# A gate argument in one VectorE step, and a new order of the work, in a fused scan and mixture-of-adapters kernel

## The chip, the cores and the metric

The kernel runs on one core of a Trainium2 chip. The metric is the device time of one execution, in microseconds, as the median of several runs. The profile is one execution taken by the hardware profiler; the engines are named PE (TensorE), DVE (VectorE), ACT (ScalarE), POOL (GpSimd) and SP (the queue that issues the loads and stores).

## The reference

Two steps are computed one after the other. A linear recurrence runs over 8 sequences of 6400 steps with 128 channels, and its outputs, 51,200 rows x of 128 values, are the tokens of a small mixture of adapters with 8 experts of rank 16, of which the two with the largest logits count:

```python
h = a[:, t] * h + b[:, t]          # scan; x[:, t] = h
logits = x @ w_gate                # [N, 8]
topk = the two largest of 8; w = softmax over these two
out = x + sum over the two of w * ((x @ A[e]) @ B[e])
```

A softmax over two logits m1 >= m2 is sigmoid(m1 - m2) for the first and sigmoid(m2 - m1) for the second. With l a logit of the row, both are sigmoid((l - m1) + (l - m2)), and for the six other experts the gate must be 0. The kernel therefore makes a gate argument that is (l - m1) + (l - m2) for the two chosen experts and hugely negative for the rest, and takes one sigmoid of it.

## The kernel before

The 51,200 rows are cut into 100 units of 512 rows. A unit w passes through these operations, whose names are those in the code:

- `ld`: SP loads a and b, mostly two units (512 KB) in one transfer, into rings of 8 slots, that is 16 units.
- `AB` (line 492): PE transposes a and b, so that channels lie on partitions and time along the free axis, into one PSUM bank each. `aev` (L526): ACT copies the bank of a to SBUF. `scan` (L550): DVE runs the recurrence, with a from SBUF and b from PSUM.
- `ZL` (L589): PE multiplies x with w_gate and A together, 136 columns for each 128 rows, three such blocks in one PSUM bank. `zl` (L607): ACT copies logits and products to SBUF.
- the gating, for a group of several units at once (below).
- `mul` (L766): the products times the gates, on POOL, 128x512, for all units but the last few, where the planner may choose DVE. `T` (L774): PE transposes the result; `tev` (L782): a copy from PSUM, on DVE in the middle of the kernel. `D` (L802): PE adds x and the product with B. `oev` (L817): ACT copies the output to SBUF. `st`: SP stores two units at a time; the store of unit u also waits for the scan of unit u + 20 (`HOLD`).

The gating of a group (the function `gating`, with tiles of 4 blocks of 8 logits for each unit of the group, so 128x96 for three units) is a chain of short operations on three engines: `m1` (DVE, largest logit), `p1` (POOL, d1 = l - m1), `r1` (ACT, a mask pn that is huge where l is the largest), `p3` (POOL, L2 = l - pn), `m2` (DVE, second largest), `p4` (POOL, d2 = l - m2), `r2` (ACT, a mask pn that is huge where l < m2), `p6` (POOL, d1 + d2), `p7` (POOL, um = d1 - pn), `sig` (ACT, g = sigmoid(um)). The first two and the last two groups are "quick": one operation per block on DVE (`mx`, L662) gives the eight logits sorted, so that m1, r1, p3 and m2 fall away, and the p steps may go to POOL or DVE.

The order in which each engine executes its instructions is not written by hand. A planner (`_Plan.schedule`) gives every operation a duration, and repeatedly picks the operation that can start first by these durations, with the `key` table of the configuration to decide between equals. Where an operation may run on two engines, it takes the one on which it starts earlier by the planner's durations. The planner also hands out the eight PSUM banks; `caps` says how many of them may be held at once by a (transposed a), b, Z (products) and O (output). Each engine then executes its list strictly in order and waits on semaphores of the other engines.

Of the kernel before, what the change touches and what calls it, by code (L numbers as in the profile page):

```python
# [5 lines left out]
ALU = mybir.AluOpType  # L6
ACTF = mybir.ActivationFunctionType
# [5 lines left out]
CFG = {  # L13
    "ring": 8,
    "xr": 20,
    "zr": 48,
    "nout": 24,
    "hold": 20,
    "heads": (1, 1, 1, 1),
    "group": 3,  # L20
    "tails": (2, 2, 1, 1),
    "quick": (2, 2),
    "split": (4, 4),
    "solo": (0, 2),
    "mul": (0, 1, 0, 8),
    "tev": (1, 1, 4, 4),
    "tail": 8,
    "fills": 5,
    "caps": {'a': 3, 'b': 4, 'Z': 1, 'O': 3, 'w': 8},
    "least": {'Z': 1, 'O': 1},  # L30
    "pairs": (98, 2),
    "ast": 3,
    "tevns": (264.0, 330.0),
    "key": {
        "AB": 170.4, "aev": 138.5, "scan": 13.3, "ZL": 157.0, "zl": 152.0, "gate": 31.6, "r1": -64.5, "r2": -65.8,
        "sig": 83.8, "mul": 73.7, "T": 119.3, "tev": 143.8, "D": 171.1, "oev": 151.4, "R": 65.1,
    },
}

# [24 lines left out]
class _Plan:  # L64
# [15 lines left out]
    def add(self, name, eng, kind, unit, busy, emit, deps=(), dma=None, mode=None, takes=(), gives=None):  # L80
        self.ops[name] = _Op(name, eng, kind, unit, busy, self.latency, emit, list(deps), dma, mode, takes, gives)
# [118 lines left out]
def bass_associative_scan_2x2__then__mixture_of_adapters_kernel(  # L200
# [8 lines left out]
    NB, S, D = a.shape  # L209
    E = moe_w_gate.shape[1]  # L210
    R = moe_A.shape[2]
# [72 lines left out]
    def z_row(block):  # L284
        return (block + shift) % ZR
# [3 lines left out]
    with ExitStack() as stack:  # L289
# [18 lines left out]
        zl = sb(nc.sbuf_tensor("zl", [128, ZR, E_A], F32))  # L308
        outt = sb(nc.sbuf_tensor("outt", [128, NOUT, UT], F32))

        def gate_tiles(name, n, shape):
            return [sb(nc.sbuf_tensor(f"{name}_{i}", [128] + shape, F32)) for i in range(n)]
# [4 lines left out]
        d1 = gate_tiles("d1", 2, [GB, E])  # L317
        L2 = gate_tiles("L2", 2, [GB, E])
        pn = gate_tiles("pn", 2, [GB, E])
        d2 = gate_tiles("d2", 2, [GB, E])  # L320
        um = gate_tiles("um", 2, [GB, E])
# [11 lines left out]
        plan = _Plan(sems, latency, 1000000.0, KEY, 100.0, len(psum), CFG["caps"], CFG["least"])  # L333
        add = plan.add

        def add_dma(name, eng, unit, starts, slot, ns, deps=(), kind="dma", issue=450.0, after=2000.0):
# [6 lines left out]
            def emit(h):  # L343
# [15 lines left out]
                out=ident_f[:, :],  # L359
# [261 lines left out]
        def gating(k):  # L621
            u0, n = groups[k]
            c = n * Q
            s = k % 2
            u = u0 + n
            quick = k < QUICK[0] or k >= len(groups) - QUICK[1]
            ge = ("pool", "dve") if quick else "pool"

            def cost(a, b):
                return {"pool": a + b * n, "dve": 70.0 + 35.0 * n}  # L630

            def v(t):
                return t[:, 0:c, :]

            r0 = z_row(u0 * Q)
            Lg = zl[:, r0 : r0 + c, 0:E]
            ready = [f"zl{i}" for w in range(u0, u0 + n) for i in fills_of[w]]

            def bc(t):
                return t[:, 0:c].to_broadcast([128, c, E])  # L640

            TT = cost(195.0, 53.5)

            def step(name, eng, time, emit, deps):
                if eng == ge:
                    time = {e: time[e] for e in ((ge,) if isinstance(ge, str) else ge)}
                add(f"{name}_{k}", eng, "gate", u, time, emit, deps)

            def relu(name, src, scale, bias, deps):
                add(  # L650
                    f"{name}_{k}",
                    "act",
                    name,
                    u,
                    103.0 + 26.7 * n,
                    lambda h: h.activation(v(pn[s]), v(src[s]), ACTF.Relu, bias=bias, scale=scale),  # L656
                    deps,
                )

            def sort(h):  # L660
                for j in range(c):
                    last = h.max(mx[s][:, j, :], Lg[:, j, :])  # L662
                return last

            if quick:
                first, second = mx[s][:, 0:c, 0], mx[s][:, 0:c, 1]
                step("mx", "dve", 20.0 + 65.0 * c, sort, ready + [f"p1_{k - 2}", f"p4_{k - 2}"])
                step(
                    "p4",
                    ge,  # L670
                    TT,
                    lambda h: h.tensor_tensor(
                        out=v(d2[s]), in0=Lg, in1=second.to_broadcast([128, c, E]), op=ALU.subtract
                    ),
                    [f"mx_{k}", f"p6_{k - 2}", f"r2_{k - 2}"],
                )
                step(
                    "p1",
                    ge,
                    TT,  # L680
                    lambda h: h.tensor_tensor(  # L681
                        out=v(d1[s]), in0=Lg, in1=first.to_broadcast([128, c, E]), op=ALU.subtract
                    ),
                    [f"mx_{k}", f"p7_{k - 2}"],
                )
            else:
                step(
                    "m1",
                    "dve",
                    44.0 + 33.4 * n,  # L690
                    lambda h: h.tensor_reduce(out=m1[s][:, 0:c], in_=Lg, axis=AX.X, op=ALU.max),
                    ready + [f"p1_{k - 2}"],
                )
                step(
                    "p1",
                    ge,
                    TT,
                    lambda h: h.tensor_tensor(out=v(d1[s]), in0=Lg, in1=bc(m1[s]), op=ALU.subtract),
                    [f"m1_{k}", f"p7_{k - 2}"],
                )  # L700
                relu("r1", d1, 1.0e30, 1.0e10, [f"p1_{k}", f"p3_{k - 2}", f"p7_{k - 2}"])
                step(
                    "p3",
                    ge,
                    TT,
                    lambda h: h.tensor_tensor(out=v(L2[s]), in0=Lg, in1=v(pn[s]), op=ALU.subtract),  # L706
                    [f"r1_{k}", f"m2_{k - 2}"],
                )
                step(
                    "m2",  # L710
                    "dve",
                    44.0 + 33.4 * n,
                    lambda h: h.tensor_reduce(out=m2[s][:, 0:c], in_=v(L2[s]), axis=AX.X, op=ALU.max),
                    [f"p3_{k}", f"p4_{k - 2}"],
                )
                step(
                    "p4",
                    ge,
                    TT,
                    lambda h: h.tensor_tensor(out=v(d2[s]), in0=Lg, in1=bc(m2[s]), op=ALU.subtract),  # L720
                    [f"m2_{k}", f"p6_{k - 2}", f"r2_{k - 2}"],
                )
            relu("r2", d2, -1.0e30, 0.0, [f"p4_{k}", f"p3_{k}", f"p7_{k - 2}"])
            step(
                "p6",
                ge,
                TT,
                lambda h: h.tensor_tensor(out=v(d1[s]), in0=v(d1[s]), in1=v(d2[s]), op=ALU.add),  # L728
                [f"p4_{k}", f"p1_{k}", f"r1_{k}"],
            )  # L730
            step(
                "p7",
                ge,
                TT,
                lambda h: h.tensor_tensor(out=v(um[s]), in0=v(d1[s]), in1=v(pn[s]), op=ALU.subtract),  # L735
                [f"r2_{k}", f"p6_{k}", f"sig{k - 2}"],
            )
            old = groups[k - 3] if k >= 3 else (0, 0)
            add(
                f"sig{k}",  # L740
                "act",
                "sig",
                u,
                104.0 + 26.7 * n,
                lambda h: h.activation(v(g[k % 3]), v(um[s]), ACTF.Sigmoid),  # L745
                [f"p7_{k}", "table"] + [f"mul{w}" for w in range(old[0], old[0] + old[1])],
            )
# [124 lines left out]
        for k in range(len(groups)):  # L872
            gating(k)
# [55 lines left out]
```

## Time and profile before

| | |
|---|---|
| time before | 202.87 us (median of 3 runs, 202.78 to 204.99) |
| span of the profiled execution | 202.7 us |
| DVE scans (L550), 512 long, with a carried start | 92, mean 1275 ns |
| POOL multiplications (L766) | 93, mean 1069 ns |
| DVE copies of zwT (L782) | 89, mean 410 ns |
| ACT masks (L656) | 72, of which 60 are 128x96 with a mean of 343 ns |
| POOL steps p1, p3, p4, p6, p7 for 128x96 | 30 each, means 354, 392, 356, 392, 394 ns |
| DVE reductions m1, m2 for 128x96 | 30 each, means 233 and 229 ns |
| DVE multiplications (L766), in the tail | 7, mean 874 ns |

Two remarks on reading it. The recorded duration of a DVE or ACT instruction overlaps the start of the next one by some 80 ns, so a group's busy time is more than what the engine's timeline grows by; the distance from start to start is the better measure of what an instruction costs. And all four engines and the DMA engines are busy for most of the span, so the busy shares alone do not say what holds the kernel.

### The profile page before, as it was taken

What the parts mean: (1) busy time and instruction counts of PE and PEld (TensorE: products, weight loads), DVE (VectorE), ACT (ScalarE), POOL (GpSimd) and SP (SyncE); (2) the same over time, 40 slices, a digit from 0 to 9 for tenths busy, and PEclk for the clock granted to TensorE, in tenths of its full rate; (3) what the DMA queues carried; (4) which work ended last, traced back from release to release, by engine and by line L of the source; (5) the groups of instructions that cost most, each with busy time, mean ns of one, the idle gap of its engine ahead of it and who ended that gap; (6) DMA issues with size and microseconds to landing.
All of it is one profiled execution on the core that took longest, in us unless ns stands there. A gap on an engine that the chain in (4) does not pass through costs nothing.

```text
span 202.7 us, 8187 instructions
## 1 busy us (share of the span) xinstructions
PE 184.9 (91%) x3204; PEld 162.4 (80%) x3204; DVE 172.1 (85%) x296; ACT 179.5 (89%) x461; POOL 157.6 (78%) x280
## 2 busy tenths in 40 slices
PE   7969999999898999998999899989999999999772
PEld 2647888889797988887898799879989889988661
DVE  1458999999999799998888888899899699798980
ACT  2248999999999998998999899999999899999863
POOL 2013678689899797888689799999999999769840
PEclk9988999999999999999999999999999999999998
DMA  6999999999999999999999999999999999975995
GB/s 206 346 417 407 409 408 405 405 407 407 410 412 412 412 416 409 412 417 413 408 411 417 410 411 413 416 413 413 416 410 411 420 408 410 395 304 216 384 407 224
DMA packets 23397, 79.30 MB, mean 391 GB/s; under 512 B 3648, under 2 KB 3776, under 8 KB 23360
## 3 DMA queue, kind: packets, MB, share of 16 engines
q1 hardware_dynamic: 22032, 78.65, 97.1%
q8 instruction: 25, 0.41, 0.8%
q10 hardware_dynamic: 1328, 0.14, 0.5%
q14 instruction: 12, 0.10, 0.1%
HBM read 52.56 MB, written 26.21 MB: 389 GB/s over the span
## 4 chain that ended last, share of the span: by engine, by line
PE 56%; ACT 20%; DVE 13%; issue 7%; POOL 1%; DVEq 0%; ACTq 0%
PE ps L492 21%; PE ps L802 15%; DVE xT L550 9%; PE ps L589 9%; PE ps L774 8%; ACT zl L607 7%; ACT a_st L526 6%; ACT outt L817 4%; DVE zw L766 2%; PE ps L401 2%; ACT pn L656 2%; DVE zwT L782 1%; PE ps L411 1%; POOL zw L766 1%; ACT g L745 1%
## 5 line engine op out<-in xcount | busy, mean ns | idle before, releaser
L550 DVE TENSOR_TENSOR_SCAN xT<-a_st,xT,ps 128x512 f16<-128x512 f32 x96 | 120.3, 1253 | 12.8 <-ACT a_st L526 5.6
L766 POOL TENSOR_TENSOR zw<-zl,g 128x512 f16<-128x512 f32 x93 | 98.9, 1069 | 9.4 <-ACT g L745 9.4
L607 ACT COPY zl<-ps 128x408 f32<-128x408 f32 (+1 forms) x139 | 71.1, 538 | 2.3 <-PE ps L589 2.3
L526 ACT COPY a_st<-ps 128x512 f32<-128x512 f32 x100 | 61.3, 637 | 10.4 <-PE ps L492 10.0
L492 PE MATMUL ps<-ident_f,a_in 64*128 64x64 f32 (+1 forms) x792 | 67.7, 230 | 3.0 <-ACT zl L607 1.0
L492 PE MATMUL ps<-ident_f,b_in 64*128 64x64 f32 (+1 forms) x792 | 67.7, 230 | 1.5 <-issue 1.5
L492 PEld LDWEIGHTS ps<-ident_f,a_in 64*128 64x128 f32 (+1 forms) x792 | 56.9, 140 | 13.2 <-issue 7.1
L817 ACT COPY outt<-ps 128x512 f32<-128x512 f32 x99 | 60.5, 627 | 2.9 <-PE ps L802 2.2
L492 PEld LDWEIGHTS ps<-ident_f,b_in 64*128 64x128 f32 (+1 forms) x792 | 56.5, 140 | 1.0 <-issue 0.9
L589 PE MATMUL ps<-cst_h,xT 128*128 128x136 f16 x400 | 49.3, 234 | 2.2 <-DVE xT L550 1.8
L802 PE MATMUL ps<-ident_h,xT 128*128 128x128 f16 x400 | 42.9, 229 | 2.3 <-issue 1.3
L774 PE MATMUL ps<-ident_h,zw 128*128 128x128 f16 x400 | 38.7, 220 | 3.7 <-DVE zw L766 2.3
L589 PEld LDWEIGHTS ps<-cst_h,xT 128*128 128x128 f16 x400 | 35.5, 148 | 6.7 <-DVE xT L550 2.9
L782 DVE COPY zwT<-ps 128x256 f32<-128x256 f32 x89 | 35.8, 410 | 3.5 <-PE ps L774 3.3
L802 PE MATMUL ps<-cst_h,zwT 128*128 128x128 f16 x400 | 38.6, 219 | 0.0
L802 PEld LDWEIGHTS ps<-ident_h,xT 128*128 128x128 f16 x400 | 33.2, 148 | 4.7 <-DVE zwT L782 1.8
L774 PEld LDWEIGHTS ps<-ident_h,zw 128*128 128x128 f16 x400 | 25.1, 98 | 7.2 <-DVE zw L766 3.2
L802 PEld LDWEIGHTS ps<-cst_h,zwT 128*128 128x128 f16 x400 | 27.2, 99 | 0.0
L656 ACT ACTIVATE pn<-d 128x96 f32<-128x96 f32 (+2 forms) x72 | 22.9, 328 | 0.1
L735 POOL TENSOR_TENSOR um<-d,pn 128x96 f32<-128x96 f32 (+2 forms) x36 | 14.2, 396 | 4.3 <-ACT pn L656 3.3
L706 POOL TENSOR_TENSOR L<-zl,pn 128x96 f32<-128x96 f32 (+2 forms) x34 | 13.4, 396 | 3.6 <-ACT pn L656 3.2
L728 POOL TENSOR_TENSOR d<-d 128x96 f32<-128x96 f32 (+2 forms) x38 | 13.9, 366 | 1.4 <-DVE d L681 0.5
(31 smaller groups left out, 87.5 us busy)
## 6 DMA issues: line engine op xcount, KB each, us to landing
a_in<-in_a_dram SPq DMA_DIRECT2D x49, 512.0 KB, 15.4
b_in<-in_b_dram SPq DMA_DIRECT2D x49, 512.0 KB, 15.5
out_dram<-outt SPq DMA_DIRECT2D x49, 512.0 KB, 15.2
a_in<-in_a_dram SPq DMA_DIRECT2D x2, 256.0 KB, 9.0
b_in<-in_b_dram SPq DMA_DIRECT2D x2, 256.0 KB, 4.5
out_dram<-outt SPq DMA_DIRECT2D x2, 256.0 KB, 2.3
cst_f<-in_moe_B_dram ACTq DMA_DIRECT2D x1, 64.0 KB, 3.6
cst_f<-in_moe_A_dram ACTq DMA_DIRECT2D x1, 64.0 KB, 10.6
```

Source lines behind the costliest of these rows:

```text
L492: last = h.transpose(*args())
L526: lambda h: h.copy(a_st[w % NAS][:, :], bank(("a", w))[:, :]),
L550: last = h.tensor_tensor_scan(out=x_at(lo, hi), data0=a_st[w % NAS][:, lo:hi], data1=bank(("b", w))[:, lo:hi], initial=init, op0=ALU.mult, ...
L589: last = h.matmul(dst, x_block((b0 + j) // Q, (b0 + j) % Q), wA_h)
L607: return h.copy(zl[:, r0 : r0 + n, :], src)
L656: lambda h: h.activation(v(pn[s]), v(src[s]), ACTF.Relu, bias=bias, scale=scale),
L735: lambda h: h.tensor_tensor(out=v(um[s]), in0=v(d1[s]), in1=v(pn[s]), op=ALU.subtract),
L766: lambda h: h.tensor_tensor(out=oview, in0=zview, in1=gview, op=ALU.mult),
L774: last = h.transpose(dst[:, q * 128 : (q + 1) * 128], zw[v % NZW][:, q, :], ident_h[:, :])
L782: return copy(zwT[v % NZT][:, :].bitcast(F32), bank(("O", v))[:, 0 : UT // 2])
L802: last = h.matmul(bank(("O", v))[:, cols], (x_block(v, q), zwT[v % NZT][:, cols])[part], (ident_h[:, :], Bcat_h)[part], start=part == 0 an ...
L817: return copy(outt[:, v % NOUT, :], bank(("O", v))[:, :])
```

## The change

The mask `r2` falls away, and with it the subtraction that applied it. In its place the gate argument is min(1e30 * (l - m2), (l - m1) + (l - m2)), computed by one DVE instruction that multiplies, compares and writes (`p7`, now always on DVE). For l < m2 the first term is hugely negative; for the two chosen experts it is not below the second. The aim is to take work from ACT and POOL and two hops from the chain of the gating.

The first mask `r1` may now run on ACT or on DVE (there as a comparison times 1e30), and `p3` on POOL or DVE, as the planner finds an earlier start. Groups hold four units instead of three, so that the gating has fewer and wider instructions. The PSUM caps, the tail settings (which of the last units may use either engine) and the key table are set anew, and with them the whole order.

```diff
-    "group": 3,
-    "tails": (2, 2, 1, 1),
+    "group": 4,
+    "flexg": (1, 0, 1),
+    "tails": (2, 2, 2, 1),
...
-    "mul": (0, 1, 0, 8),
-    "tev": (1, 1, 4, 4),
-    "tail": 8,
+    "mul": (0, 1, 0, 10),
+    "tev": (1, 1, 6, 6),
+    "tail": 12,
...
-    "caps": {'a': 3, 'b': 4, 'Z': 1, 'O': 3, 'w': 8},
+    "caps": {'a': 2, 'b': 4, 'Z': 1, 'O': 4, 'w': 8},
...
-            def relu(name, src, scale, bias, deps):
-                add(
-                    f"{name}_{k}",
-                    "act",
...
-                    lambda h: h.activation(v(pn[s]), v(src[s]), ACTF.Relu, bias=bias, scale=scale),
...
+            def relu(name, src, deps):
+                big = ("act", "dve") if CFG["flexg"][2] else ("act",)
+
+                def emit(h):
+                    if plan.ops[f"{name}_{k}"].eng == "act":
+                        return h.activation(v(pn[s]), v(src[s]), ACTF.Relu, bias=1.0e10, scale=1.0e30)
+                    return h.tensor_scalar(v(pn[s]), v(src[s]), 0.0, 1.0e30, op0=ALU.is_ge, op1=ALU.mult)
+
+                time = {"act": 103.0 + 26.7 * n, "dve": 70.0 + 18.0 * n}
+                add(f"{name}_{k}", big, name, u, {e: time[e] for e in big}, emit, deps)
...
                 step(
                     "p3",
-                    ge,
+                    ("pool", "dve") if CFG["flexg"][0] else ge,
...
-            relu("r2", d2, -1.0e30, 0.0, [f"p4_{k}", f"p3_{k}", f"p7_{k - 2}"])
...
             step(
                 "p7",
-                ge,
-                TT,
-                lambda h: h.tensor_tensor(out=v(um[s]), in0=v(d1[s]), in1=v(pn[s]), op=ALU.subtract),
-                [f"r2_{k}", f"p6_{k}", f"sig{k - 2}"],
+                "dve",
+                75.0 + 35.0 * n,
+                lambda h: h.scalar_tensor_tensor(
+                    out=v(um[s]), in0=v(d2[s]), scalar=1.0e30, in1=v(d1[s]), op0=ALU.mult, op1=ALU.min
+                ),
+                [f"p6_{k}", f"sig{k - 2}"],
             )
```

More of the change, by code (lines that the diff above doesn't have):

```diff
@@ L34 @@
     "key": {
-        "AB": 170.4, "aev": 138.5, "scan": 13.3, "ZL": 157.0, "zl": 152.0, "gate": 31.6, "r1": -64.5, "r2": -65.8,
-        "sig": 83.8, "mul": 73.7, "T": 119.3, "tev": 143.8, "D": 171.1, "oev": 151.4, "R": 65.1,
+        "AB": 181.7, "aev": 221.2, "scan": 202.0, "ZL": 172.7, "zl": 171.7, "gate": 204.9, "r1": 174.3, "sig": 123.7,
+        "mul": 240.8, "T": 181.5, "tev": 215.6, "D": 121.9, "oev": 218.3, "r2": 120.0, "R": 65.1,
     },
@@ L644, in step @@
             def step(name, eng, time, emit, deps):
-                if eng == ge:
-                    time = {e: time[e] for e in ((ge,) if isinstance(ge, str) else ge)}
+                if isinstance(time, dict):
+                    time = {e: time[e] for e in ((eng,) if isinstance(eng, str) else eng)}
                 add(f"{name}_{k}", eng, "gate", u, time, emit, deps)
-            def relu(name, src, scale, bias, deps):
-                add(
-                    f"{name}_{k}",
-                    "act",
-                    name,
-                    u,
-                    103.0 + 26.7 * n,
-                    lambda h: h.activation(v(pn[s]), v(src[s]), ACTF.Relu, bias=bias, scale=scale),
-                    deps,
-                )
+            def relu(name, src, deps):
[6 more added lines that the diff above has]
+                add(f"{name}_{k}", big, name, u, {e: time[e] for e in big}, emit, deps)
             def sort(h):
@@ L674, in gating @@
                     ),
-                    [f"mx_{k}", f"p6_{k - 2}", f"r2_{k - 2}"],
+                    [f"mx_{k}", f"p7_{k - 2}"],
                 )
@@ L700, in gating @@
                 )
-                relu("r1", d1, 1.0e30, 1.0e10, [f"p1_{k}", f"p3_{k - 2}", f"p7_{k - 2}"])
+                relu("r1", d1, [f"p1_{k}", f"p3_{k - 2}"])
                 step(
                     "p3",
-                    ge,
+                    ("pool", "dve") if CFG["flexg"][0] else ge,
                     TT,
@@ L720, in gating @@
                     lambda h: h.tensor_tensor(out=v(d2[s]), in0=Lg, in1=bc(m2[s]), op=ALU.subtract),
-                    [f"m2_{k}", f"p6_{k - 2}", f"r2_{k - 2}"],
+                    [f"m2_{k}", f"p7_{k - 2}"],
                 )
-            relu("r2", d2, -1.0e30, 0.0, [f"p4_{k}", f"p3_{k}", f"p7_{k - 2}"])
             step(
                 "p6",
-                ge,
+                ge if quick or CFG["flexg"][1] == 0 else ("pool", "dve"),
                 TT,
@@ L732, in gating @@
                 "p7",
-                ge,
-                TT,
-                lambda h: h.tensor_tensor(out=v(um[s]), in0=v(d1[s]), in1=v(pn[s]), op=ALU.subtract),
-                [f"r2_{k}", f"p6_{k}", f"sig{k - 2}"],
+                "dve",
[4 more added lines that the diff above has]
+                [f"p6_{k}", f"sig{k - 2}"],
             )
```

## The prediction, made before the run

> **What bounds the kernel now.** I read the table of busy time by stretch first, because the shares over the whole span (DVE 85%, ACT 89%, PE 91%) hide that the stages differ. Columns: window, length, busy time (and instructions) of PE, PEld, DVE, ACT, POOL, then granted clock, DMA share, GB/s.
>
> ```profile
> 20.00:40.00 20.00, 19.02 (x371) 16.74 (x369) 19.20 (x27) 19.70 (x56) 14.24 (x31) 1.00 1.03 407
> 40.00:60.00 20.00, 19.02 (x357) 17.16 (x353) 19.70 (x32) 19.41 (x51) 18.62 (x33) 1.00 1.03 409
> 100.00:120.00 20.00, 18.78 (x335) 17.13 (x336) 16.83 (x29) 19.29 (x50) 17.72 (x32) 1.00 1.03 412
> ...
> 160.00:175.00 15.00, 14.79 (x282) 13.80 (x281) 14.66 (x25) 14.43 (x37) 13.83 (x23) 1.00 1.03 411
> 175.00:186.30 11.30, 10.88 (x185) 9.67 (x182) 9.93 (x18) 11.07 (x30) 9.37 (x17) 1.00 0.72 287
> 186.30:199.60 13.30, 9.55 (x132) 7.86 (x132) 10.18 (x30) 10.38 (x31) 8.06 (x15) 1.00 0.88 347
> ```
>
> Three things are to be seen. From 20 to 175 us the DMA engines are saturated at 407 to 414 GB/s. From 20 to 60 us DVE is busy 38.9 of 40 us: scans run ahead at loading speed. From 60 to 160 us DVE has room (88.5 busy of 100 us by the same table), and from 175 us the DMA rate drops, though stores are left. The waits of the DMA queue after 160 us say what those stores wait for:
>
> ```profile
> SPq L193 <- DVE xT L550: 19.3, 7, 4.2
> ```
>
> That is the rule that a store waits for the scan 20 units later. The last scan starts at 185.1 us and ends at 186.3; from there 16.4 us of outputs and stores follow. So the end is set by when compute, the scans above all, gets through. The DMA floor lies lower: 79.3 MB at 412 GB/s take 192.5 us; with 3.3 us lost to the slower first two slices (206 and 346 GB/s of 5.07 us each) and 2 us from the last issue to landing, about 198 us.
>
> **What a DVE instruction costs here.** From start to start in the order of time (start, duration):
>
> ```profile
> 164.79 1.27 DVE L550 TENSOR_TENSOR_SCAN xT<-a_st,xT,ps 128x512 f16<-128x512 f32 x1
> 165.98 0.22 DVE L713 TENSOR_REDUCE m<-L 128x12 f32<-128x96 f32 x1
> 166.13 0.41 DVE L782 COPY zwT<-ps 128x256 f32<-128x256 f32 x1
> 166.46 1.26 DVE L550 TENSOR_TENSOR_SCAN xT<-a_st,xT,ps 128x512 f16<-128x512 f32 x1
> ...
> 190.93 0.68 DVE L766 TENSOR_TENSOR zw<-zl,g 128x512 f16<-128x512 f32 x1
> 191.53 0.28 DVE L735 TENSOR_TENSOR um<-d,pn 128x32 f32<-128x32 f32 x1
> ...
> 192.98 0.19 DVE L681 TENSOR_TENSOR d<-zl,mx 128x32 f32<-128x32 f32 x1
> 193.08 0.68 DVE L817 COPY outt<-ps 128x512 f32<-128x512 f32 x1
> ```
>
> A scan takes 1.19 us, a reduction of 96 elements 0.15, a copy 0.33, a two-input operation 0.10 for 32 elements and 0.60 for 512, hence by the slope of 1.04 ns per element 0.20 for 128.
>
> **What the kernel hardly shows yet.** Two-input DVE operations beside POOL occur only at the ends. There (min, median and max ns, then the order of time):
>
> ```profile
> L766 DVE TENSOR_TENSOR zw<-zl,g x7: 673/693/1543, 188.4 to 196.5; 128x512 f16<-128x512 f32 x7
> L766 POOL TENSOR_TENSOR zw<-zl,g x93: 1052/1064/1509, 18.2 to 193.9; 128x512 f16<-128x512 f32 x93
> ```
>
> ```profile
> 193.69 2.23 DVE L766 TENSOR_TENSOR zw<-zl,g 128x512 f16<-128x512 f32 x2
> ...
> 193.86 1.51 POOL L766 TENSOR_TENSOR zw<-zl,g 128x512 f16<-128x512 f32 x1
> ```
>
> DVE starts a multiplication at 193.69; POOL's starts at 193.86 and is lengthened by 0.45 us; DVE's second is lengthened by 0.85 (1543 against 693) until POOL is through. They take turns as wholes, and a POOL `mul` keeps DVE out for up to about 0.85 us. [...] scans of 512 stay at 1273 ns in the median and 1282 at most, although POOL multiplies beside them. [...]
>
> **The change part by part.** The order of the changed program gives the counts.
>
> *ACT.* 62 masks fewer (72 to 10) at 0.18 us from start to start (173.39 to 173.57), 7 sigmoids fewer, 3 copies and one output more: about 11 us less of 179.5.
>
> *POOL.* `p7` goes (36 records, 14.2 us), and `p3` shrinks from 34 records (13.5 us) to 4; the other three steps become wider and fewer (34 to 38 of each become 29 to 31). About 30 us less of 157.6. `mul` stays at 93 and PE's work at 3204 matmuls.
>
> *DVE, plain cost.* `p3` 21 wide and 2 small: 4.4 us. `p7` 22 wide, 3 of 64 at 0.14, 6 small: 5.4; it is a two-input pass that no row shows, taken like the others (0.17 to 0.25). `r1` 14 wide, 3 smaller: 0.10 (the 32-element floor) to 0.20 [...] I take 0.14: 2.3 us. The reductions, 60 of 96 becoming 44 of 128 (0.185 each), 0.6 less. Three copies, one output and four small steps less, four sorted blocks more: 1.7 less. Sum +9.8 us on 172.1.
>
> *DVE, new blocking.* 71 of its operations (17 `r1`, 23 `p3`, 31 `p7`) now meet POOL. Bounds: 0 each if POOL always rests, 0.85 each if a `mul` has always just begun. For a random arrival: 93 multiplications, 1.03 us from start to start, [...] are 79 us of about 205, a chance of 0.385 times half of 0.85: 0.165 us each, 12 us together. I take this. In the new order `p3` comes one copy (0.33 us) after `r1`, and `r1` waits for `p1`, after which POOL has three multiplications queued: that pair will often meet the next `mul` with 0.5 us left, while `p7` follows `p6`, when POOL's next step needs an `m1` that stands behind `p7`, and so may find POOL idle.
>
> *Waits that move.* `p7` and `r1` stand in DVE's list waiting for POOL (`p6`, `p1`); behind each are a copy (PE waits for its bank in `D`) and the next scan (PE and the stores wait). Before, these waits were on POOL's and ACT's lists. The caps cost nothing that I can price: PE's waits for ACT banks are 1.0 us for `zl`, and two banks of a outlast an `aev` of 0.48 us.
>
> *By stage*, with the counts of the order for scans 8 to 33, 34 to 85 and 86 to 99:
> - 20 to 60 us: 5 each of `r1`, `p3`, `p7` wide, 2 small: 2.9 plain, 0.1 less for reductions, 15 x 0.165 = 2.5 of blocking: 5.3 against 1.1 us idle, of which half stays: +4.8.
> - 60 to 160 us: 7, 12 and 13 wide: 6.0, less 0.7 for reductions and 1.3 for copies, blocking 32 x 0.165 = 5.3: 9.3 into 11.5 us of idle, of which 2.8 stay (the idle share of the stage before): +0.6.
> - 160 to 186 us: 2, 4 and 4 wide, three small: 2.3 plain, 1.8 blocking into 1.7 us idle, 0.7 of which stays: +3.1. ACT and PE are as full there, but relief of ACT does not help while DVE has more to do than time.
> - The tail: 13 outputs instead of 11 stand behind the last `aev` (0.7 us of PE for each), against one hop less (`r2`, 0.23 us and its signal) in three small groups and a freer POOL: 0.
>
> Sum +8.5: **211 us**, slower by 4%.
>
> **Rivals.**
> 1. *The blocking hardly bites* (POOL, 30 us freer, rests when DVE comes). Then the stages give +2.3, 0 and +1.3: 206.5, less some 2 us as ACT no longer fills 175 to 186 us: 204.5, within 2%. For it: `p7` after `p6`. Against it: `mul` alone takes 47% of the time, and `p3` sits in its midst.
> 2. *The relief of ACT and POOL wins.* ACT is at 97% from 100 to 186 us, its `a_st` holds up scans for 11.1 us and `g` holds up POOL for 9.4. If DVE packs at 97% without blocking, the DMA dip from 175 us closes and the floor is met: 198. Against it: DVE would have to be busy for 182 us of some 185 between its first scan at 7.3 us and its last copy.
> 3. *The pair of `r1` and `p3` meets `mul` nearly each time* (0.69 us for the pair, by 0.165 + 0.52), and delays in DVE's list upset the order on the others: twice the blocking and some bubbles, 218.
>
> **How the numbers follow.** Main case 0.50, rival one 0.25, rival two 0.12, rival three 0.13. The main case spreads by some 4 us, so a tenth of it falls below 206.9 (2%): slower 0.58, same 0.30, faster 0.12. The range leaves out rival two and the far end of three: 200.5 to 218.
>
> **What would show it.** Right: `p3` and `r1` on DVE with means well over their 0.28 and 0.22 us and single ones near 1.0; DVE over 93% busy, ACT near 168 and POOL near 128; PE and SP waiting longer for scans; DMA below 400 GB/s before 175 us. Wrong: wide DVE steps all at 0.28 us (no blocking), or an idle DVE between 60 and 160 us, or the last scan before 186 us.

## The result and the profile after

The changed kernel takes 213.64 us (median of 4 runs, 212.67 to 214.78) against 203.0 us: a ratio of 1.0505 with a 95% interval of 1.0431 to 1.0578. It is 5% slower. Every time from here on is the median of the executions outside a slower state that some of them fall into, so the 211.3 us which one expectation quotes, with such an execution counted in, is 210.2 us in the text. The profiled execution spans 213.0 us; it was the longest of the four (the others span 210.6 to 211.4 us).

First the table of busy time by stretch, read as before (window, length, busy time and instructions of PE, PEld, DVE, ACT, POOL, clock, DMA share, GB/s), from the changed kernel:

```profile
20.00:40.00 20.00, 18.56 (x340) 15.91 (x336) 19.75 (x29) 18.37 (x46) 11.92 (x21) 1.00 1.03 408
40.00:60.00 20.00, 18.03 (x319) 16.14 (x319) 19.87 (x34) 16.78 (x38) 14.82 (x20) 1.00 1.02 408
100.00:120.00 20.00, 18.33 (x339) 16.66 (x335) 19.87 (x33) 16.94 (x38) 14.02 (x18) 1.00 1.03 413
160.00:175.00 15.00, 13.02 (x233) 11.69 (x233) 14.96 (x27) 13.35 (x30) 11.36 (x16) 1.00 1.00 399
175.00:186.30 11.30, 10.71 (x155) 9.82 (x157) 10.44 (x19) 8.86 (x20) 7.59 (x10) 0.85 0.44 176
```

DVE is the fullest engine now: 19.87 of 20 us from 100 to 120, where it had 16.83. ACT and POOL have fallen to 16.9 and 14.0. DMA keeps its rate nearly to 175 us and then breaks down to 176 GB/s, while the stores wait longer for scans (29.5 us instead of 19.3):

```profile
SPq L194 <- DVE xT L551: 29.5, 10, 5.6
```

The waits of the engines (total us, times, longest) say what the relieved engines do with their time. For the most part they wait for DVE, directly or a step behind it:

```profile
POOL zw L768 <- ACT g L747: 23.4, 22, 2.2
POOL d L721 <- DVE m L714: 13.9, 22, 1.6
ACT a_st L527 <- PE ps L493: 12.2, 14, 2.0
POOL d L699 <- DVE m L692: 12.1, 13, 1.6
ACT a_st L527 <- DVE xT L551: 9.0, 9, 1.3
```

`g` is one step behind `p7` on DVE; before, POOL waited 9.4 us for it. The granted clock of 0.85 in the last row of the table is that of a stretch at half clock (0.50 from 176 to 178 us). The profiled execution of the kernel before has one too, but from 14 to 16 us, where the first loads still come in. So a part of what this execution lost after 175 us may be its own. What fills DVE is to be seen in the groups of instructions by shape (line, engine, operation, tiles, count, then busy us and mean ns):

```profile
L707 DVE TENSOR_TENSOR L<-zl,pn 128x128 f32<-128x128 f32 x21 | 15.1, 719 | 1.0 <-ACT pn L655 0.9
L656 DVE TENSOR_SCALAR pn<-d 128x128 f32<-128x128 f32 x14 | 8.2, 587 | 0.0
L735 DVE SCALAR_TENSOR_TENSOR um<-d 128x128 f32<-128x128 f32 x22 | 6.1, 277 | 0.0
```

Three operations on the same 128 elements: `p7` takes 277 ns, `p3` 719 and `r1`, which reads one input only, 587. The order of time shows why, first DVE, then POOL in the same stretch (start, duration):

```profile
101.05 0.77 DVE L656 TENSOR_SCALAR pn<-d 128x128 f32<-128x128 f32 x1
101.74 0.41 DVE L784 COPY zwT<-ps 128x256 f32<-128x256 f32 x1
102.07 0.83 DVE L707 TENSOR_TENSOR L<-zl,pn 128x128 f32<-128x128 f32 x1
102.82 1.27 DVE L551 TENSOR_TENSOR_SCAN xT<-a_st,xT,ps 128x512 f16<-128x512 f32 x1
...
107.25 0.26 DVE L735 SCALAR_TENSOR_TENSOR um<-d 128x128 f32<-128x128 f32 x1
107.44 0.28 DVE L692 TENSOR_REDUCE m<-zl 128x16 f32<-128x128 f32 x1
```

```profile
100.67 3.15 POOL L768 TENSOR_TENSOR zw<-zl,g 128x512 f16<-128x512 f32 x3 [0.56 <-ACT g L747]
...
105.85 0.46 POOL L728 TENSOR_TENSOR d<-d 128x128 f32<-128x128 f32 x1
107.79 0.41 POOL L699 TENSOR_TENSOR d<-zl,m 128x128 f32<-128x128 f32 x1 [1.48 <-DVE m L692]
```

POOL's three multiplications begin at 100.67 and 1.05 us apart, so they end near 101.7, 102.8 and 103.8. `r1` comes in the midst of the first and ends as that ends; `p3` comes in the midst of the second and ends as that ends. The copy between them, which reads PSUM, keeps its 0.41 us. `p7` at 107.25 finds POOL resting (its next step at 107.79 needs the `m1` behind `p7`) and takes 0.26.

### The profile page after: what moved, and what is told of

The parts are those of the page before. It is cut to its first block, busy times and chain, and to the rows that moved or that the text cites. A ratio compares the mean times of both kernels' runs of the same rounds, so it can differ in the third digit from the quotient of the medians.

```text
span 213.0 us, 8033 instructions
## 1 busy us (share of the span) xinstructions
PE 188.6 (89%) x3204; PEld 166.1 (78%) x3204; DVE 193.8 (91%) x349; ACT 174.9 (82%) x396; POOL 135.2 (63%) x195
## 4 chain that ended last, share of the span: by engine, by line
DVE 36%; PE 36%; DMA 11%; issue 7%; ACT 6%; POOL 2%; SPq 1%; ACTq 0%; DVEq 0%
DVE xT L551 22%; PE ps L493 12%; PE ps L804 12%; DMA b_in<-in_b_dram 11%; PE ps L590 6%; PE ps L776 6%; DVE zwT L784 5%; DVE L L707 4%; ACT a_st L527 2%; DVE um L735 2%; ACT zl L608 2%; ACT outt L819 2%; DVE pn L656 1%; SPq L346 1%; DVE m L692 1%
## 5 line engine op out<-in xcount | busy, mean ns | idle before, releaser
L768 POOL TENSOR_TENSOR zw<-zl,g 128x512 f16<-128x512 f32 x93 | 98.5, 1077 | 25.5 <-ACT g L747 23.4
L527 ACT COPY a_st<-ps 128x512 f32<-128x512 f32 x100 | 57.5, 599 | 22.2 <-PE ps L493 12.2
L608 ACT COPY zl<-ps 128x408 f32<-128x408 f32 (+1 forms) x139 | 65.9, 499 | 2.3 <-PE ps L590 1.5
L819 ACT COPY outt<-ps 128x512 f32<-128x512 f32 x100 | 57.3, 596 | 5.1 <-PE ps L804 4.4
L590 PE MATMUL ps<-cst_h,xT 128*128 128x136 f16 x400 | 48.2, 234 | 1.5 <-DVE xT L551 0.6
L804 PE MATMUL ps<-ident_h,xT 128*128 128x128 f16 x400 | 45.4, 236 | 4.5 <-DVE zwT L784 4.2
L776 PE MATMUL ps<-ident_h,zw 128*128 128x128 f16 x400 | 37.0, 221 | 4.4 <-ACT a_st L527 1.8
L784 DVE COPY zwT<-ps 128x256 f32<-128x256 f32 x86 | 33.9, 410 | 1.2 <-PE ps L776 1.2
L721 POOL TENSOR_TENSOR d<-zl,m 128x128 f32<-128x128 f32 (+2 forms) x27 | 11.4, 421 | 14.7 <-DVE m L714 13.9
L699 POOL TENSOR_TENSOR d<-zl,m 128x128 f32<-128x128 f32 (+2 forms) x27 | 10.3, 383 | 13.7 <-DVE m L692 12.1
L707 DVE TENSOR_TENSOR L<-zl,pn 128x128 f32<-128x128 f32 (+1 forms) x23 | 15.5, 672 | 1.0 <-ACT pn L655 0.9
L728 POOL TENSOR_TENSOR d<-d 128x128 f32<-128x128 f32 (+2 forms) x31 | 12.7, 408 | 1.9 <-DVE d L682 0.5
```

What stands on the lines that cost most here:

```text
L527: lambda h: h.copy(a_st[w % NAS][:, :], bank(("a", w))[:, :]),
L590: last = h.matmul(dst, x_block((b0 + j) // Q, (b0 + j) % Q), wA_h)
L608: return h.copy(zl[:, r0 : r0 + n, :], src)
L768: lambda h: h.tensor_tensor(out=oview, in0=zview, in1=gview, op=ALU.mult),
L776: last = h.transpose(dst[:, q * 128 : (q + 1) * 128], zw[v % NZW][:, q, :], ident_h[:, :])
L784: return copy(zwT[v % NZT][:, :].bitcast(F32), bank(("O", v))[:, 0 : UT // 2])
```

## The experiments

The theory, L: DVE is full, and its two-input operations and `r1` (one input; that it is blocked too was the author's estimate) stand blocked beside POOL's multiplications. The rivals: O, the wider groups, caps and new order cost the time; P, the plain DVE work does, blocked or not; later S, the order that the planner makes for a set of operations. Each ratio (with its 95% interval) is against runs of the kernel before on the same chip.

**The whole change but the two steps that moved.**

```diff
-    "flexg": (1, 0, 1),
+    "flexg": (0, 0, 0),
```

> Edit: the changed kernel with flexg (0, 0, 0): r1 always on ScalarE, p3 always on GpSimd; p7 stays on VectorE, groups of 4, caps and keys as changed. Theory L (VectorE is full, and p3 and r1 stand blocked there by GpSimd's multiplications): VectorE loses 23 p3 and 17 r1, some 21 us from start to start, and ends near 173 us busy; the time falls to 200 to 204 us. Theory O (the wider groups, the caps and the new order are what costs): the time stays at 210 us or more. Theory P (the plain VectorE work of all three steps, without blocking): p3 and r1 are worth only their plain 7 us, so about 206 to 208 us.

206.49 us, ratio 1.017 (1.0126 to 1.0215). Most of the loss goes, but not all: L had said 200 to 204, and the time lies in the range of P (206 to 208). This run alone does not tell the two apart. DVE is busy 178.3 us instead of 193.8. `p7` now has a mean of 423 ns, not 277: in the lists made for this set it meets multiplications (a later run tests this).

**One step at a time.** The same with `(1, 0, 0)`, 20 of 27 `p3` on DVE:

> Edit: flexg (1, 0, 0): p3 may go to VectorE (20 of 27 do), r1 always on ScalarE. Theory L: 20 p3 at 0.20 plain plus 0.2 to 0.45 of blocking are 8 to 13 us on VectorE; time 205 to 209 us, p3 with a mean of 0.5 us or more. Theory P: 4 us more than without p3, so within 2 us of the kernel that has neither; p3 near 0.28 us. Theory O: 210 us or more.

207.41 us, 1.0215 (1.0166 to 1.0263), which both L and P had allowed. And with `(0, 0, 1)`, 21 of 27 `r1` on DVE:

> Edit: flexg (0, 0, 1): r1 may go to VectorE (21 of 27 do), p3 always on GpSimd. Theory L[...]: 21 r1 at 0.14 plain plus 0.2 to 0.4 of blocking, 7 to 11 us; time 204 to 208 us, r1 with a mean of 0.4 us or more. If such an operation is not blocked: r1 near 0.2 us and 201 to 204 us. Theory O: 210 us or more.

208.04 us, 1.0245 (1.022 to 1.0269), at the end of L's range. Means of 645 ns for `p3` and 605 ns for `r1` (128 wide) show both blocked, the one-input operation too. `p3` alone adds only 0.9 us to the 206.5 and `r1` alone 1.5, both together 7.1. DVE's busy time rises by 7.9, 6.6 and 15.5 us; the first part fits into its slack and the rest does not. That reading is argued from these numbers; no run isolates it, and each of the sets has lists of its own.

**The same lists with a POOL that reads nothing.** This is the sharpest test: what an instruction does, not where it stands, is changed.

```diff
+                if plan.ops[f"mul{v}"].eng == "pool":
...
+                        last = h.memset(zw[v % NZW][:, :, :], 0.0)
...
-                lambda h: h.tensor_tensor(out=oview, in0=zview, in1=gview, op=ALU.mult),
+                emit,
```

> Edit: the changed kernel with its order and its VectorE list untouched, but the 93 GpSimd multiplications are memsets of the same 128x512 tile, which read nothing from SBUF. Left out: the products times the gates (the adapters' part of the output). Theory L: with no reading GpSimd instruction beside them p3 falls from a mean of 0.72 us to about 0.3; r1 falls from 0.59 to about 0.2 [...], and less than that [...]; VectorE loses 9 to 15 us; time 200 to 206 us. Theory P (the plain work counts): VectorE's list is the same, so 210 us or more.

203.21 us, 1.0014 (0.9971 to 1.0057): the loss is gone. But this memset is also shorter (533 ns for 1077), so the next run makes it 1024 elements long:

> Edit: as the run with memsets, but each GpSimd memset covers 1024 elements (the tile made twice as long), so that GpSimd is busy nearly as long per unit as with the multiplication. The order of all engines is that of the changed kernel. Left out: the products times the gates. Theory L (blocking by reading GpSimd instructions costs the time): p3 stays near 0.28 us, r1 stays blocked in part, as in the shorter memset, and the time stays at 203 to 206 us. Rival R (what helped was the freer GpSimd, 47 us instead of 98 for the multiplications): the time goes back to 209 us or more.

205.26 us, 1.0107 (1.0044 to 1.017), with POOL's memsets busy 87.0 us where the multiplications took 98.5. 8.4 us of the 10.6 are gone with POOL nearly as busy. The `p3` line of the changed kernel and then of this run (min, median, max ns):

```profile
L707 DVE TENSOR_TENSOR L<-zl,pn x23: 176/828/1168, 19.0 to 189.6; 128x128 f32<-128x128 f32 x21, 128x32 f32<-128x32 f32 x2
```

```profile
L707 DVE TENSOR_TENSOR L<-zl,pn x23: 181/283/294, 18.1 to 179.7; 128x128 f32<-128x128 f32 x21, 128x32 f32<-128x32 f32 x2
```

Not one `p3` is above 294 ns. `r1` is still blocked in part, as expected: its mean is 742 ns, against 399 beside the shorter memsets and the 0.20 us of one that met nothing on POOL (at 27.39 us in the changed kernel). R, which said 209 or more, is refuted, and P too, since DVE's list is the same. Some 2 us do come back with the longer memsets (ratio 1.0107 for 1.0014); the longer blocking of `r1` is a likely reason, but no run isolates it. PE multiplies zeros in these runs, and its granted clock is hardly another: 0.993 here and 0.991 in the changed kernel.

**The control on the kernel before**, with the same long memsets:

> Edit: the kernel before with the same long memsets in place of GpSimd's multiplications; left out the same products. Its VectorE has two-input operations only in the first and last units. Theory L: within 1% of the kernel before (201 to 204 us). Rival R2 (a GpSimd that does not read helps any order, through other engines): 199 us or less.

203.27 us, 0.9999 (0.9962 to 1.0036). A POOL that does not read is worth nothing here, where DVE has no two-input work in the middle.

**The new gate argument alone, and the order alone.** The first takes the kernel before and swaps `r2` and the old `p7` for the one DVE instruction; the second takes the old gating with the new configuration (groups of four, tails, caps, keys).

> Edit: the kernel before (groups of three, its caps, tails and keys) with the new gate argument alone: r2 gone, p7 one VectorE instruction, r1 on ScalarE and p3 on GpSimd. Theory L: 38 p7 at 0.2 us plain and 0.1 to 0.2 of blocking are 10 to 14 us more on VectorE, of which the slack from 60 to 160 us takes most; ScalarE loses 6.5 us, GpSimd 14: 201 to 205 us. Theory O (the wider groups, caps and keys cost the 3 us that the version with r1 and p3 off VectorE still lost): 201 to 203 us, clearly under that version's 206.5.

210.22 us, 1.0365 (1.029 to 1.0441).

> Edit: the old gating (r1 and r2 on ScalarE, p3 and p7 on GpSimd) with the changed kernel's groups of four, caps, tails and keys. Theory L: VectorE has no two-input operation in the middle, so no blocking; ScalarE has 58 masks; 201 to 205 us. Theory O: 206 us or more, as much as the version with r1 and p3 off VectorE.

203.36 us, 1.0016 (0.9992 to 1.004). O is refuted: with the old gating, the new groups, caps, tails and keys cost nothing. The new gate argument alone was a clear miss: I expected 201 to 205. Its `p7` has a mean of 506 ns, which is blocking again, but is that all? The same lists with write-only memsets:

> Edit: the run with the new gate argument alone (groups of three), its order untouched, with GpSimd's multiplications replaced by write-only memsets of 1024 elements. Left out: the products times the gates. There p7 had a mean of 506 ns and the time was 211.3 us. Theory L: p7 falls to 0.24 us and the time to 202 to 205 us. Rival S (the order that the planner makes for this set is poor, by the lists themselves): 208 us or more.

208.86 us, 1.0249 (1.0154 to 1.0343). `p7` falls to 251 ns, but the ratio only from 1.0365 to 1.0249, so the time is where S had put it. The order of time on DVE near the end of this run shows a likely cause:

```profile
183.81 1.27 DVE L551 TENSOR_TENSOR_SCAN xT<-a_st,xT,ps 128x512 f16<-128x512 f32 x1
...
187.87 0.25 DVE L735 SCALAR_TENSOR_TENSOR um<-d 128x96 f32<-128x96 f32 x1
188.89 0.69 DVE L764 TENSOR_TENSOR zw<-zl,g 128x512 f16<-128x512 f32 x1 [0.77 <-ACT g L747]
189.50 1.27 DVE L551 TENSOR_TENSOR_SCAN xT<-a_st,xT,ps 128x512 f16<-128x512 f32 x1
```

The planner put the last scan behind copies, reductions, a `p7` and a multiplication that waits for `g`: 5.7 us lie between the last two scans (1.9 in the kernel before), and the last stores wait for that scan. In the profiled executions nearly the whole loss arises there: the last scan but one starts at 183.81 us (183.16 in the kernel before), the last at 189.50 (185.05), and what follows it takes 16.6 us (16.4). So the lists of the changed kernel mend something that has nothing to do with blocking. A run of this set with only the last scan moved was not made, so that this place is the cause is read from the traces and not tested.

**The remaining 3 us of the first experiment**, by its lists with write-only memsets:

> Edit: the run with r1 and p3 off VectorE, its order untouched, with the same write-only memsets; same products left out. There p7 had a mean of 423 ns and the time was 206.5 us. Theory L: p7 falls to 0.27 us and the time to 202 to 204 us, so that the 3 us which that version still lost were p7's blocking. Rival S: 206 us or more.

203.93 us, 1.0014 (0.9981 to 1.0047), with `p7` at 284 ns. With `r1` and `p3` off DVE, what still was lost was the blocking of `p7`. The plain work of the new `p7` is all there in this run, and beside what the change saves on ACT and POOL it costs nothing that shows.

**Shorter multiplications.** If POOL keeps DVE out for a whole instruction, two halves keep it out half as long each:

```diff
+                    for q in range(0, Q, 2):
+                        last = h.tensor_tensor(
+                            out=oview[:, q : q + 2], in0=zview[:, q : q + 2], in1=gview[:, q : q + 2], op=ALU.mult
+                        )
```

> Edit: the changed kernel, all lists as they are, but each GpSimd multiplication is issued as two of 128x256; nothing is left out. GpSimd gets some 15 to 20 us more work, and has over 50 us of waits. Theory L[...]: what a VectorE instruction can wait falls from 0.85 to about 0.45 us; p3 from a mean of 0.72 to 0.45 to 0.6, r1 from 0.59 to 0.35 to 0.5, 4 to 7 us less on VectorE; time 207 to 211 us. Rival B ([...] element by element): p3 and r1 stay as they are and the time does not fall below 213 us.

208.29 us, 1.0258 (1.0225 to 1.0291): 5.3 us faster than the changed kernel (whose ratio is 1.0505), with nothing left out and more work on POOL.

```profile
L764 POOL TENSOR_TENSOR zw<-zl,g 128x256 f16<-128x256 f32 x186 | 111.9, 631 | 23.3 <-ACT g L747 21.6 <-PE ps L786 1.3
L707 DVE TENSOR_TENSOR L<-zl,pn 128x128 f32<-128x128 f32 x21 | 9.8, 467 | 0.6 <-ACT pn L655 0.5
L656 DVE TENSOR_SCALAR pn<-d 128x128 f32<-128x128 f32 x14 | 5.2, 374 | 0.0
```

`p3` falls from 719 to 467, `r1` from 587 to 374. Rival B, by which the two engines share element by element, had both stay as they were.

**The plain work by itself**, in the kernel before:

```diff
+                h.tensor_reduce(out=spare[:, k, i, 0:c], in_=src, axis=AX.X, op=ALU.max)
+                return h.tensor_reduce(out=dst, in_=src, axis=AX.X, op=ALU.max)
```

> Edit: the kernel before, each of the 64 reductions m1 and m2 done twice, the first into a spare tile; all other lists as they are. This is 64 x 0.15 = 9.6 us more on VectorE, of a kind that reads one input [...], about as much as the plain cost in the prediction (9.8). By the prediction's stages without blocking: +2 to +4 us, 204 to 207 us. Rival (the plain work alone makes the loss): 210 us or more.

204.9 us, 1.0077 (1.0041 to 1.0112): some 9.6 us of unblocked DVE work (DVE's busy time rises by 8.1) cost some 1.6 us. P is refuted a second time. The slack did absorb most of it (20 to 160 us, the run and then the kernel before):

```profile
20.00:60.00 40.00, 38.36 (x703) 33.68 (x700) 39.30 (x72) 38.75 (x101) 32.33 (x60) 1.00 1.03 408
60.00:160.00 100.00, 95.37 (x1745) 86.29 (x1744) 93.47 (x185) 95.52 (x241) 89.53 (x150) 1.00 1.03 413
```

```profile
20.00:60.00 40.00, 38.05 (x720) 33.91 (x717) 38.90 (x58) 39.12 (x106) 32.85 (x63) 1.00 1.03 408
60.00:160.00 100.00, 94.56 (x1735) 86.13 (x1732) 88.49 (x150) 95.62 (x243) 89.89 (x151) 1.00 1.03 413
```

No version tried is shown to beat the kernel before; the new configuration with the old gating equals it.

## Why the prediction was right

The direction, the cause and the size held: 211 was forecast, 213.6 measured, within the range. That the sum came so close is in part luck: the blocking was put too low and the plain work too high. By its steps:

- *The end hangs on the last scan.* Right. It ends at 195.8 us instead of 186.3 (+9.5), and 17.2 us follow instead of 16.4 (+0.8; I had 0; two small `p7` there met multiplications and took 1.08 and 0.82 us). The sum is the 10.3 us between the spans.
- *The blocking.* Right in kind (the runs with write-only memsets and with halves), short in size: I took 0.165 us for each of 71 operations, 12 us (from the 0.85 us of the one meeting in the tail; that `r1` is among them was an estimate). Against their unblocked durations 21 wide `p3` lost 0.44 us each (719 against 282), 9.2 us; 14 wide `r1` about 0.39 (587 against the 0.20 us of the one that met nothing on POOL), 5.4; the small `p7` 1.6 and the 22 wide ones 0.2: 16 us. A random arrival was the wrong picture for both ends: 15 of the 21 wide `p3` wait for a multiplication under way, mostly the one that began as `r1` ended, and of the 22 wide `p7` only one meets one (479 ns). The prediction had named both and not put them into the sum.
- *The plain work.* Mis-sized the other way. I gave it 3.6 us (2.3, 0 and 1.3 by stage), with 0.14 us for `r1` as an estimate that no row had shown; 9.6 us of another unblocked kind cost 1.6.
- *The stages.* At 60 us the changed kernel has begun two scans fewer, at 160 us three and at 180 us five. From 60 to 160 us a scan begins every 1.8 us or so; that makes some 4, 2 and 4 us for the three stages, so the first and third carry most of the loss, as said; I gave them 4.8 and 3.1 us and the middle 0.6. A part of the third may be the stretch at half clock.
- *Rivals.* The blocking that hardly bites is refuted, and the relief of ACT and POOL that wins is refuted even with most of the blocking gone: with memsets of half the length the time was 203.2, not 198. So the relief bought nothing; in the changed kernel the freed engines wait for DVE, and why nothing was won with the memsets stays open. The third rival's pair of `r1` and `p3` was real, its 218 us too much.
- *Signs that I named.* Single `p3` and `r1` near 1.0 us: right (1168 and 1011 ns). DVE over 93%, ACT near 168 and POOL near 128: wrong (91%, 174.9, 135.2); busy time counts overlapping records once, and as ACT and POOL are packed less tightly, more of the 80 ns overlaps count in full (argued). DMA below 400 GB/s before 175 us: wrong but for 399 from 160 to 175. SP waiting longer for scans: right (29.5 us instead of 19.3); PE: wrong (its matrix multiplications of `ZL` waited 0.6 us for scans, before 1.8). Loads run up to 16 units ahead, so a late scan does not starve the DMA engines before the loads run out; then it does (413 GB/s from 100 to 120 us, 176 from 175; argued).

What had not been foreseen is that the new gate argument on its own, with the old groups, would cost some 7 us (ratio 1.0365), of which most (1.0249) stays without blocking and is put down to the lists.

## What to carry to other kernels

Before moving a two-input operation from GpSimd or ScalarE to VectorE, look at what GpSimd runs at that moment: here a 0.2 us step cost 0.75 us beside a 1 us multiplication, and the shares of busy time of the kernel before showed nothing of it. Such a step waited until the GpSimd instruction was through (15 of the 21 wide `p3`), so where the two must run together, shorter GpSimd instructions can be the better ones although they add work: halves won 5.3 us here. Relief of an engine need not be worth anything: 22 us less on GpSimd and 5 us less on ScalarE won nothing while VectorE was full. And where a planner sets the order, an edit is to be judged together with the lists that it makes: here the new gate argument, with `r1` and `p3` off VectorE, cost some 7 us with one configuration and some 3.5 us with another.

## What the hardware showed that was not expected

- A long record of the one-input `tensor_scalar` beside write-only memsets did not mean that it held DVE as long. In the run with long memsets `r1` starts at 103.00 and is recorded for 0.68 us, yet the next copy starts 0.12 us later and both end at 103.68:

```profile
103.00 0.68 DVE L656 TENSOR_SCALAR pn<-d 128x128 f32<-128x128 f32 x1
103.12 0.56 DVE L792 COPY zwT<-ps 128x256 f32<-128x256 f32 x1
103.72 0.29 DVE L707 TENSOR_TENSOR L<-zl,pn 128x128 f32<-128x128 f32 x1
```

  The pair takes 0.72 us from start to start; unblocked the copy alone takes 0.33 (107.63 to 107.96 in the changed kernel). So the mean of 742 ns may overstate what the run lost; where `p3` comes next, though, it waits for the whole mask (1.82 us from start to start at 162.17 us).
- The `scalar_tensor_tensor` with multiply and minimum cost no more than a plain two-input operation: in that run its mean is 269 ns for 128 elements against 282 for `p3`, both unblocked.
- Cutting POOL's 93 multiplications in two costs 13.4 us of POOL's busy time (111.9 for 98.5), 0.14 us for each, and the kernel gets faster by it.
- A one-input `tensor_scalar` on 128 elements that met nothing on POOL was recorded for 0.20 us (the `r1` at 27.39 us in the changed kernel); less the overlap of some 80 ns that is an estimate of 0.12 from start to start. The two-input `p7` was recorded for 0.26 and took 0.19 from start to start (at 107.25 us there). No row of the kernel before had shown the first.
